# Linear attention with the values as weights and the keys moving on column quarters, products of three steps grouped by tile shape

## The chip, the cores and the metric

The kernel runs on one core of a Trainium2 chip. The metric is the device time of one execution in microseconds (us). Three runs of the kernel before took 985.79, 983.8 and 984.3 us, median 984.3. Engines are named as in the profile: PE (matmul), PEld (weight load, beside PE), DVE, ACT, POOL, and SP, which issues transfers.

## What is computed

Linear attention over 4 batches and 8 heads (576 positions, head size 64, 128 features), then a max-of-three feed-forward layer, then a noisy top-2 mixture of eight experts. Only the attention changes:

```python
def phi(x):
    proj = np.einsum('bhsd,df->bhsf', x, w_phi)
    proj = proj - np.max(np.abs(proj), axis=-1, keepdims=True)
    return np.concatenate([np.exp(proj), np.exp(-proj)], axis=-1)
q_p, k_p = (phi(q), phi(k))
kv = np.einsum('bhsf,bhsd->bhfd', k_p, v)
z = np.sum(k_p, axis=2)
num = np.einsum('bhsf,bhfd->bhsd', q_p, kv)
den = np.einsum('bhsf,bhf->bhs', q_p, z)[..., None] + 1e-06
return (num / den).astype(np.float32)
```

## The kernel before, in words

Attention runs as 16 steps, one for each batch and pair of heads. A step `s` has these parts, each a function:

- `turn` (L388) transposes keys or queries on PE into PSUM, `raw_in` (L398) copies them out on ACT to `th`, and `proj` (L409) multiplies by `w_phi`, 64 rows of the array for each head of the pair. Kind "k" is the keys, "q" the queries, "r" the last 64 positions of two steps together, done on even steps.
- `peak` (L419) and `center` (L434) take the largest absolute value off on DVE, giving `d`. `exp_k` (L446) makes the key features `kp` on ACT. `turn_q` (L452) transposes `d` of the queries on PE, and `exp_q` (L461) makes the query features `qp` from it on ACT.
- `kv_sum` (L481) sums key features times values. The key features are the weights, 128 by 128, and 128 columns move: two value heads of 64, of which one is the ones column block, so that the sum `z` comes out of the same product. One step has 20 such products. `kv_out` (L486) copies the sum to `kv`.
- `denom` (L514) and `numer` (L497) apply it to the query features, 288 positions at a time; `denom` on 32-column quarters of the array, `numer` on 64-column halves.
- `den_in` (ACT), `den_turn` (L529), `den_inv` (L535), `den_copy` (L542), `den_back` (L546) and `divide` (L552, all DVE) end the step and write `xT`.

Beside this, `narrow_mid` (L186, L195 on DVE, L198 on ACT) and `narrow_end` (POOL, four passes) turn 64-bit weights of the next layer into 32-bit ones, 24 halves in all; `narrow_load` (L175) brings their `bits` by DMA.

All order is one list of pairs (time, function), sorted by time: `period` adds the parts of one step at `base + t`, `opening` those before it, and the lines behind `B0` those of the last step, which are mixed with the first products of the next layer (L768). The times are only sort keys. Every engine works its own list in that order, so a waiting instruction holds up all that stands behind it on its engine. PE's results go to eight PSUM banks, named s (3), t (2), p (2) and k (1).

Of the kernel before, what the change touches and what calls it, by code (L numbers as in the profile page):

```python
# [38 lines left out]
def tile_linear_attention__then__moe__then__noisy_top2_moe(  # L39
# [336 lines left out]
    def turn(s, kind):  # L376
# [12 lines left out]
        st["raw", kind] = pt[:, :n]  # L389
# [11 lines left out]
    def proj(s, kind, banks=(bank_p, bank_p)):  # L401
# [3 lines left out]
        pj = [bank().rearrange("p (a f) -> p a f", a=4) for bank in banks]  # L405
# [42 lines left out]
    def turn_q(s, kind, g):  # L448
        pt = bank_t().rearrange("p (a c) -> p a c", a=4)
# [19 lines left out]
    def kv_sum(s, h, part=None):  # L469
        u, i, bb, hp = heads(s)  # L470
        if h == 0 and not part:
            st["pkv"] = bank_k().rearrange("p (a f) -> p a f", a=4)

        order = [(sg, j) for sg in range(2) for j in range(JT)] + [(0, JT), (1, JT)]
        cuts = (0, JT, 2 * JT, len(order))
        for sg, j in order if part is None else order[cuts[part]:cuts[part + 1]]:
            if j < JT:
                kp, vv = kps[s][:, j % 2, 2 * h + j // 2, sg, :], tiles[s][2][:, j, h:h + 2, :]
            else:
                kp, vv = kps[u, "r"][:, h, sg, :], vls[i][:, hp, h:h + 2, :]  # L480
            nc.tensor.matmul(st["pkv"][:, 2 * h + sg, :], kp, vv.rearrange("p a d -> p (a d)"),  # L481
                             start=(j == 0 and sg == 0), stop=(j == JT and sg == 1))

    def kv_out(s):
        kv = ap.tile([P, 4, P], F32, name="kv", bufs=2)
        nc.scalar.activation(kv, st.pop("pkv"), AF.Copy)  # L486
        st["kv", s] = kv

    def numer(s, n, bank=bank_s):
        u, i, bb, hp = heads(s)
        p_ = bank()[:, :HALF]
        for sg in range(2):
            for h in range(2):
                nc.tensor.matmul(p_[h * D:(h + 1) * D], st["kv", s][:, 2 * h + sg, h * D:(h + 1) * D],  # L497
                                 qps[u, i][:, h, sg, n * HALF:(n + 1) * HALF],
                                 start=(sg == 0), stop=(sg == 1))
# [8 lines left out]
    def denom(s, bank=bank_s):  # L508
        u, i, bb, hp = heads(s)
        p_ = bank()[:, :HALF]  # L510
        for sg in range(2):
            for n in range(2):
                for h in range(2):
                    nc.tensor.matmul(p_[quarter(h, n)],  # L514
                                     st["kv", s][:, 2 * h + sg, (1 - h) * D:(1 - h) * D + QD],
# [40 lines left out]
    STEP = 12.5  # L556
# [43 lines left out]
    def period(base, a, b):  # L600

        def at(t, f, *x):
            plan.at(base + t, f, *x)

        if 0 < a < NS:
# [8 lines left out]
        if a < NS and a % 2 == 0:  # L614
            at(0.0, prepare, a)
        if 1 < a < NS:
            if a + 1 == 2 * HP:
                at(0.0, load_rest, 1)
            at(0.0, turn, a, "k")
            at(0.5, raw_in, a, "k")  # L620
            at(2.7, turn, a, "q")
            at(3.2, raw_in, a, "q")
            at(3.15, proj, a, "k")
            at(4.0, peak, a, "k", 0)
            at(4.7, center, a, "k", 0)
            at(5.4, peak, a, "k", 1)
            at(6.1, center, a, "k", 1)
            for g in range(2):
                for sg in range(2):
                    at(5.3 + 1.5 * g + 0.6 * sg, exp_k, a, "k", g, sg)  # L630
            at(7.25, proj, a, "q")
        if 0 < a < NS:
            at(8.1, peak, a, "q", 0)
            at(8.8, center, a, "q", 0)
            at(9.5, peak, a, "q", 1)
            at(10.2, center, a, "q", 1)
            at(9.95, turn_q, a, "q", 0)
            at(10.5, exp_q, a, "q", 0)
            at(11.05, turn_q, a, "q", 1)
            at(11.5, exp_q, a, "q", 1)  # L640
            if a % 2 == 0:
                at(2.8, turn, a, "r")
                at(3.4, raw_in, a, "r")
                at(11.4, proj, a, "r")
                for g in range(2):
                    at(11.5 + 0.01 * g, peak, a, "r", g)
                    at(11.52 + 0.01 * g, center, a, "r", g)
                at(STEP + 3.0, turn_q, a, "r", 0)
                at(STEP + 3.1, exp_q, a, "r", 0)
                at(12.39, exp_k, a, "r", 0, 0)  # L650
                at(12.39, exp_k, a, "r", 0, 1)
        if a < NS:
            for i, n in enumerate(step_halves(a)):
                if i:
                    at(7.6, narrow_high, n)
                    at(11.15, narrow_low, n)
                    at(11.3, narrow_end, n)
                    at(STEP + 4.0, narrow_out, n)
                    continue
                at(1.8 if a > 1 else 11.0, narrow_mid, n)  # L660
                at(2.8 if a > 1 else 11.5, narrow_end, n)
                at(STEP + (1.6 if a > 1 else 9.0), narrow_out, n)
            for n in step_halves(a + 1):
                at(8.0, narrow_load, n)
            if a:
                at(10.5, kv_sum, a, 0, 0)
        if 0 < b:
            at(4.05, numer, b - 1, 1)
            at(6.9, divide, b - 1, 1)
            at(0.45, kv_sum, b, 0, 1)  # L670
            at(2.75, kv_sum, b, 0, 2)
            at(5.0, kv_sum, b, 1)
            if b + 1 == 2 * HP:
                at(7.3, load_rest_v, 1)
            at(7.3, kv_out, b)
        if 0 <= b:
            at(8.15, denom, b)
            at(9.1, numer, b, 0)
            at(9.15, den_in, b)
            at(10.9, den_turn, b)  # L680
            at(11.0, den_inv, b)
            for n in range(2):
                at(11.05, den_copy, b, n)
                at(11.8 + 0.5 * n, den_back, b, n)
            at(11.9, divide, b, 0)

    def opening():

        at(1.2, busy, 12)
        at(4.0, turn, 0, "k")  # L690
        at(4.45, raw_in, 0, "k", True)
        at(4.5, busy, 3)
        at(5.2, proj, 0, "k")
        at(6.3, turn, 0, "r")
        at(6.6, raw_in, 0, "r")
        at(6.6, turn, 0, "q")
        at(7.1, raw_in, 0, "q")
        at(7.2, proj, 0, "r", (bank_s, bank_s))
        at(7.7, proj, 0, "q", (bank_p, bank_s))
        at(9.0, turn, 1, "k")  # L700
        at(9.6, raw_in, 1, "k")
        at(9.7, busy, 4)
        for g in range(2):
            at(6.4 + 1.4 * g, peak, 0, "k", g)
            at(7.1 + 1.4 * g, center, 0, "k", g)
            at(9.3 + 0.01 * g, peak, 0, "r", g)
            at(10.0 + 0.01 * g, center, 0, "r", g)
            at(10.8 + 1.4 * g, peak, 0, "q", g)
            at(11.5 + 1.4 * g, center, 0, "q", g)
            at(13.6 + 1.4 * g, peak, 1, "k", g)  # L710
            at(14.3 + 1.4 * g, center, 1, "k", g)
            for sg in range(2):
                at(8.0 + 1.3 * g + 0.6 * sg, exp_k, 0, "k", g, sg)
                at(15.4 + 2.8 * g + 0.6 * sg, exp_k, 1, "k", g, sg)
        for sg in range(2):
            at(10.7 + 0.4 * sg, exp_k, 0, "r", 0, sg)
        at(11.2, kv_sum, 0, 0)
        at(12.5, turn_q, 0, "r", 0)
        at(12.6, turn, 1, "q")
        at(13.0, exp_q, 0, "r", 0)  # L720
        at(13.2, raw_in, 1, "q")
        at(13.3, proj, 1, "k")
        at(13.8, turn_q, 0, "q", 0)
        at(14.3, exp_q, 0, "q", 0)
        at(14.3, kv_sum, 0, 1)
        at(16.6, kv_out, 0)
        at(16.6, turn_q, 0, "q", 1)
        at(17.1, exp_q, 0, "q", 1)
        at(17.1, proj, 1, "q")
# [3 lines left out]
    for s in range(NS):  # L733
# [1016 lines left out]
```

## Time and profile before

| | us |
|---|---|
| median of three runs | 984.3 |
| the profiled execution's own time | 983.95 |
| its span, first to last instruction | 982.4 |
| PE busy | 972.4 |
| DVE busy | 587.3 |
| ACT busy | 449.7 |
| POOL busy | 489.8 |

The attention takes the first 220 us of the span or so; the two later layers fill the rest. A matmul of 32-bit numbers shows as two records, each with its own weight load, and each lasts longer than the time to the next one's start. So PE's rate is read from starts, not from durations.

### The profile page before, as it was taken

To read this page: it belongs to the slowest core of one execution; us is meant where nothing else is said; L and a number is where in the kernel's file an instruction comes from. 1 tells how busy PE (TensorE), PEld (TensorE's weight loads), DVE (VectorE), ACT (ScalarE), POOL (GpSimd) and SP (SyncE) were. 2 spreads that over 40 slices of the span, in tenths; PEclk is the share of its full clock that TensorE was granted. 3 is DMA by queue.
4 is the path that set the end of the run, shared out by engine and by line. 5 is a ranking of instruction groups with operands and counts; after the bars stand their busy time and mean duration, and the time that the engine had idled before them with its cause. 6 is when DMAs were issued, how large, how long until landed. Compare 5 with 4: busy or idle time off the path is not lost. (4 is left out here: it accounts for less than half of the span.)

```text
span 982.4 us, 17094 instructions
## 1 busy us (share of the span) xinstructions
PE 972.4 (99%) x6285; PEld 852.0 (87%) x6285; DVE 587.3 (60%) x1253; ACT 449.7 (46%) x878; POOL 489.8 (50%) x554
## 2 busy tenths in 40 slices
PE   9999999999999999999999999999999999999997
PEld 7777777779999999999998789989898989889895
DVE  5889888886344363636355525557577665756641
ACT  5666666554233433334335414337364554546350
POOL 2767655582137464545323553137474655647252
PEclk9999999999999999999999999999999999999999
DMA  6547666345155657565516264728475565748312
GB/s 187 147 137 194 186 202 183 119 129 163 47 167 173 220 162 236 176 218 184 178 30 199 55 203 153 293 85 302 143 271 199 203 229 174 279 130 315 113 33 71
DMA packets 125352, 169.08 MB, mean 172 GB/s; under 512 B 35630, under 2 KB 86958, under 8 KB 125266
## 3 DMA queue, kind: packets, MB, share of 16 engines
q1 hardware_dynamic: 114338, 138.35, 45.0%
q0 software_dynamic: 10928, 29.62, 8.7%
q8 instruction: 50, 0.82, 0.3%
q14 instruction: 36, 0.29, 0.1%
HBM read 119.38 MB, written 49.14 MB: 172 GB/s over the span
## 5 line engine op out<-in xcount | busy, mean ns | idle before, releaser
L768 PE MATMUL s<-xh,wh 128*128 128x384 f32 x432 | 147.9, 342 | 0.3 <-DVE a L778 0.3
L768 PE MATMUL s<-xh,wl 128*128 128x384 f32 x432 | 145.3, 336 | 0.0
L768 PE MATMUL s<-xl,wh 128*128 128x384 f32 x432 | 145.1, 336 | 0.0
L1229 POOL DMA_INDIRECT out_dram<-o,emeta x40 | 47.1, 1178 | 130.9 <-DVE o L1227 67.3
L778 DVE TENSOR_TENSOR a<-s,a 128x384 f32<-128x384 f32 x72 | 40.0, 555 | 91.7 <-PE s L768 89.7
L1302 DVE TENSOR_TENSOR wl<-raw,wh 128x1024 fp32r<-128x1024 f32 x58 | 70.8, 1220 | 26.5 <-ACT wh L1294 25.8
L768 PEld LDWEIGHTS s<-xh,wh 128*128 128x128 f32 x432 | 81.1, 188 | 6.2 <-DVE a L778 2.5
L1219 PE MATMUL p<-wh,hh 128*128 128x512 f32 (+1 forms) x216 | 86.4, 400 | 0.0
L1219 PE MATMUL p<-wl,hh 128*128 128x512 f32 (+1 forms) x216 | 85.3, 395 | 0.0
L1219 PE MATMUL p<-wh,hl 128*128 128x512 f32 (+1 forms) x216 | 85.2, 395 | 0.0
L768 PEld LDWEIGHTS s<-xl,wh 128*128 128x128 f32 x432 | 81.2, 188 | 1.5
L768 PEld LDWEIGHTS s<-xh,wl 128*128 128x128 f32 x432 | 81.1, 188 | 0.0
L1294 ACT ACTIVATE wh<-raw 128x1024 fp32r<-128x1024 f32 x58 | 61.2, 1056 | 31.3 <-DMA raw<-in_moe_w_dram 16.5
L1272 POOL TENSOR_TENSOR raw<-raw 128x256 f32<-128x256 f32 x24 | 20.4, 849 | 105.5 <-DMA raw<-in_moe_w_dram 90.5
L481 PEld LDWEIGHTS k<-vt,kp 128*128 128x128 f32 x512 | 60.8, 192 | 6.9 <-issue 6.5
L481 PE MATMUL k<-vt,kp 128*128 128x128 f32 x512 | 66.5, 278 | 0.1
L419 DVE TENSOR_REDUCE m<-p 128x4 f32<-128x512 f32 (+1 forms) x77 | 48.5, 637 | 27.9 <-PE p L409 27.8
L944 POOL DMA_INDIRECT meta<-mt,si x36 | 36.7, 1020 | 56.4 <-DVE si L940 47.3
L206 POOL TENSOR_TENSOR nm<-nm,nr 128x512 int32<-128x512 int32 x24 | 30.5, 1273 | 66.2 <-ACT nr L198 35.2
L1077 PE MATMUL s<-gx,wh 128*128 128x304 f32 x288 | 62.1, 302 | 0.0
L127 DVE TENSOR_TENSOR gx<-t,gx 128x512 fp32r<-128x512 f32 (+3 forms) x82 | 39.5, 496 | 32.9 <-ACT gx L126 32.4
L126 ACT ACTIVATE hh<-a 128x384 fp32r<-128x384 f32 x36 | 18.8, 522 | 87.9 <-DVE a L778 84.6
(279 smaller groups left out, 2552.7 us busy)
## 6 DMA issues: line engine op xcount, KB each, us to landing
raw<-in_moe_w_dram SPq DMA_DIRECT2D x58, 512.0 KB
raw<-in_moe_w_dram SPq DMA_DIRECT2D x48, 256.0 KB
sums<-qh SPq DMA_DIRECT2D x24, 512.0 KB
sums<-raw SPq DMA_DIRECT2D x24, 512.0 KB
wh<-sums SPq DMA_DIRECT2D x24, 512.0 KB
wl<-sums SPq DMA_DIRECT2D x24, 512.0 KB
bits<-in_moe_w_dram SPq DMA_DIRECT2D x18, 512.0 KB
out_dram<-zrow SPq DMA_DIRECT2D x9, 512.0 KB
```

The costliest lines, as they stand in the source:

```text
L127: nc.vector.tensor_tensor(lo, src, hi.bitcast(F32), op=ALU.subtract)
L206: nc.gpsimd.tensor_tensor(m_, m_, r_, op=ALU.add)
L419: nc.vector.tensor_reduce(m, st["pj", kind, g][:, :n], axis=AX.X, op=ALU.max, apply_absolute_value=True)
L481: nc.tensor.matmul(st["pkv"][:, 2 * h + sg, :], kp, vv.rearrange("p a d -> p (a d)"), start=(j == 0 and sg == 0), stop=(j == JT and sg == 1))
L768: nc.tensor.matmul(p_, a[:, d, fs], b_, start=(n == 0), stop=(n == 3 * KD - 1))
L778: nc.vector.tensor_tensor(a, p_, st.pop("a"), op=ALU.max)
L944: ins = nc.gpsimd.indirect_dma_start(out=meta, out_offset=bass.IndirectOffsetOnAxis(ap=si[:, t, kk:kk + 1], axis=0), in_=mt[:, t, kk, :], ...
L1077: nc.tensor.matmul(bk["p"], a[:, d, fs], b_[:, d, :], start=(d == 0 and i == 0), stop=(d == 1 and i == 2))
L1219: nc.tensor.matmul(p_, a, b_[:, fw], start=(f == 0 and r == 0), stop=(f == (3 if seven(n) else F2 - 1) and r == 2))
L1229: alone(e, nc.gpsimd.indirect_dma_start(out=out, out_offset=bass.IndirectOffsetOnAxis(ap=mt[:m, i, 1:2], axis=0), in_=o[:m], in_offset=Non ...
L1294: nc.scalar.activation(WE[e, i][0], st["w2", e, i], AF.Copy)
L1302: nc.vector.tensor_tensor(wl, st.pop(("w2", e, i)), wh.bitcast(F32), op=ALU.subtract)
```

## The change

`kv_sum` now takes 32 columns of the values as weights and moves the key features, 256 columns at a time (both signs), on the four column quarters of the array at once. `z_sum` does the same with 32 columns of ones and 128 moving columns. The result stands turned: `kv_out` copies it to `kvT`, and `kv_turn` (three transposes on PE) and `kv_in` (ACT) turn it back into `kv`. `numer` now works on 32-column quarters, as `denom` did. `period(a)` holds the projections of step a, `turn_q`, `kv_sum` and `z_sum` of step a-1, and `denom` and `numer` of step a-2, each kind of array shape in one run; every PSUM use names its bank. On odd steps from 3 two halves of `narrow` are done instead of on even ones.

```diff
-        pt = bank_t().rearrange("p (a c) -> p a c", a=4)
+        pt = bank(name).rearrange("p (a c) -> p a c", a=4)
...
-            d = ap.tile([P, 4, NF], F32, name="d", bufs=3)
+            d = ap.tile([P, 4, NF], F32, name=f"d{kind}", bufs=2)
...
-        order = [(sg, j) for sg in range(2) for j in range(JT)] + [(0, JT), (1, JT)]
-        cuts = (0, JT, 2 * JT, len(order))
-        for sg, j in order if part is None else order[cuts[part]:cuts[part + 1]]:
-            if j < JT:
-                kp, vv = kps[s][:, j % 2, 2 * h + j // 2, sg, :], tiles[s][2][:, j, h:h + 2, :]
-            else:
-                kp, vv = kps[u, "r"][:, h, sg, :], vls[i][:, hp, h:h + 2, :]
-            nc.tensor.matmul(st["pkv"][:, 2 * h + sg, :], kp, vv.rearrange("p a d -> p (a d)"),
-                             start=(j == 0 and sg == 0), stop=(j == JT and sg == 1))
+    def kv_sum(s):
+        st["pkv"] = bank("k")[:, :3 * P]
+        for j, vv, kp in chunks(s):
+            for c in range(4):
+                h, cs = c // 2, slice(c * QD, (c + 1) * QD)
+                nc.tensor.matmul(st["pkv"][cs, :2 * P], vv[:, 2 * h, c % 2 * QD:(c % 2 + 1) * QD],
+                                 kp[h].rearrange("p g f -> p (g f)"), start=(j == 0), stop=False,
+                                 tile_position=(0, cs.start))
+
+    def z_sum(s):
+        for j, vv, kp in chunks(s):
+            for c in range(4):
+                cs = slice(c * QD, (c + 1) * QD)
+                nc.tensor.matmul(st["pkv"][cs, 2 * P:], vv[:, 1, :QD], kp[c // 2][:, c % 2], start=False,
+                                 stop=(j == JT), tile_position=(0, cs.start))
...
+    def kv_turn(s, name):
+        t = st.pop(("kvT", s))
+        pt = bank(name)[:, :3 * P]
+        for j in range(3):
+            nc.tensor.transpose(pt[:, j * P:(j + 1) * P], t[:, j * P:(j + 1) * P], ident)
...
-            for h in range(2):
-                nc.tensor.matmul(p_[h * D:(h + 1) * D], st["kv", s][:, 2 * h + sg, h * D:(h + 1) * D],
+            for c in range(4):
+                cs = slice(c * QD, (c + 1) * QD)
+                nc.tensor.matmul(p_[cs], st["kv", s][:, sg, cs],
...
-    STEP = 12.5
+    STEP = 10.9
...
-            return min(a, 1) + (a % 2 == 0 or a == NS - 1 if a > 2 else 0)
+            return min(a, 1) + (a % 2 if a > 2 else 0)
...
+        at(0.0, turn, a, "k", A_)
+        at(0.44, turn, a, "q", B_)
+            at(0.88, kv_turn, c, D_)
+        at(1.2, turn_q, b, "q", 0, C_)
+            at(1.65, turn, a, "r", G_)
+        at(1.9, turn_q, b, "q", 1, E_)
+        at(2.35, proj, a, "k", (A_, B_))
+        at(3.25, proj, a, "q", (C_, D_))
+            at(4.15, proj, a, "r", (G_, H_))
+        at(4.6, kv_sum, b)
+        at(6.8, z_sum, b)
+        at(8.0, kv_out, b)
+            at(7.9, denom, c, E_)
+            at(8.9, numer, c, 0, G_)
+            at(9.9, numer, c, 1, H_)
+            den_steps(10.1, c, at)
...
+        at(4.3, turn, 0, "q", C_)
+        at(4.5, turn, 0, "r", G_)
+        at(5.0, proj, 0, "k", (A_, B_))
+        at(5.3, proj, 0, "q", (C_, D_))
+        at(5.5, proj, 0, "r", (G_, H_))
```

The first place where order counts is PE in the middle of the attention. Before, a step with its two turns for "q" stands so (`t<-ident,d` is `turn_q`, `p<-wphi` is `proj`, `k<-v` is `kv_sum`, `s<-qp,kv` is `denom` with 32 and `numer` with 64 columns):

```order
L514 MATMUL s<-qp_160,kv 32x288 x8
L497 MATMUL s<-qp_160,kv 64x288 x4
L452 MATMUL t<-ident,d 128x128 x4
L481 MATMUL k<-vt_110,kp_509 128x128 x4
L452 MATMUL t<-ident,d 128x128 x4
L409 MATMUL p<-wphi,th 128x128 x4
L388 MATMUL t<-ident,km 128x128 x4
L481 MATMUL k<-vt_110,kp_509 128x128 x4
L388 MATMUL t<-ident,qm 128x128 x4
L481 MATMUL k<-vl_111,kp_606 128x128 x2
L452 MATMUL t<-ident,d 128x128 x2
L409 MATMUL p<-wphi,th 128x128 x8
```

Now, from the end of one period to the first projection of the next (L486 is `kv_sum`, L494 `z_sum`, L535 `denom`, L520 `numer`, L392 `turn`, L506 `kv_turn`, L456 `turn_q`, L413 `proj`):

```order
L494 MATMUL k<-kp_516,vt_110 32x128 x16
L494 MATMUL k<-kp_552,vl_111 32x128 x4
L535 MATMUL t_779<-qp_260,kv 32x288 x8
L520 MATMUL s_796<-qp_260,kv 32x288 x8
L520 MATMUL t_813<-qp_260,kv 32x288 x8
L392 MATMUL p_837<-ident,km 128x128 x4
L392 MATMUL p_844<-ident,qm 128x128 x4
L506 MATMUL s_853<-ident,kvT 128x128 x3
L456 MATMUL s_860<-ident,dq 128x128 x4
L392 MATMUL s_874<-ident,kl 128x128
L392 MATMUL s_874<-ident,ql 128x128
L456 MATMUL t_879<-ident,dq 128x128 x4
```

What changed shape seven to nine times in a step changes it three times: 32-column products, transposes, 64-row projections.

The second place is DVE between the last `center` of one step and the first `peak` of the next, before and now:

```order
L434 TENSOR_TENSOR d<-p,m 128x512
L529 STREAM_TRANSPOSE dt<-dn 128x288
L535 RECIPROCAL rc<-dt 128x18
L542 COPY rc<-rc 32x9 x4
L546 STREAM_TRANSPOSE rb<-rc 128x288
L552 TENSOR_TENSOR xT<-s,rb 128x288
L546 STREAM_TRANSPOSE rb<-rc 128x288
L186 TENSOR_SCALAR nm<-bits 128x512
L195 SCALAR_TENSOR_TENSOR nm<-bits,nm 128x512
L419 TENSOR_REDUCE m<-p 128x4
```

```order
L438 TENSOR_TENSOR dq<-s_710,m 128x512
L550 STREAM_TRANSPOSE dt<-dn 128x288
L556 RECIPROCAL rc<-dt 128x18
L563 COPY rc<-rc 32x9 x4
L567 STREAM_TRANSPOSE rb<-rc 128x288
L573 TENSOR_TENSOR xT<-s_796,rb 128x288
L190 TENSOR_SCALAR nm<-bits 128x512
L199 SCALAR_TENSOR_TENSOR nm<-bits,nm 128x512
L567 STREAM_TRANSPOSE rb<-rc 128x288
L573 TENSOR_TENSOR xT<-t_813,rb 128x288
L423 TENSOR_REDUCE m<-p_887 128x4
```

The instructions are the same; both divisions now stand here, where one stood between the key and query projections of the next step.

## Rows read from the trace of the kernel before

**Rows 1.** The page's first part: busy time, share of the span, instructions.

```profile
PE 972.4 (99%) x6285; PEld 852.0 (87%) x6285; DVE 587.3 (60%) x1253; ACT 449.7 (46%) x878; POOL 489.8 (50%) x554
```

**Rows 2.** Windows: length; busy (instructions) of PE, PEld, DVE, ACT, POOL; PEclk, DMA share, GB/s.

```profile
32.49:203.22 170.73, 170.10 (x1643) 132.17 (x1643) 141.97 (x301) 109.68 (x232) 108.31 (x85) 1.00 0.58 166
0.00:12.00 12.00, 9.92 (x79) 7.48 (x80) 5.29 (x13) 5.64 (x11) 6.59 (x34) 1.00 0.48 127
```

**Rows 3.** PE in order of time: start, us, form, records.

```profile
98.70 1.18 PE L514 MATMUL s<-qp,kv 128*32 128x288 f32 x16
99.81 1.19 PE L497 MATMUL s<-qp,kv 128*64 128x288 f32 x8
...
101.42 1.06 PE L481 MATMUL k<-vt,kp 128*128 128x128 f32 x8
102.31 0.60 PE L452 MATMUL t<-ident,d 128*128 128x128 f32 x4
102.76 0.66 PE L388 MATMUL t<-ident,km 128*128 128x128 f32 x4
...
109.98 1.16 PE L409 MATMUL p<-wphi,th 64*128 64x128 f32 x16
111.07 1.18 PE L514 MATMUL s<-qp,kv 128*32 128x288 f32 x16
...
124.83 1.18 PE L514 MATMUL s<-qp,kv 128*32 128x288 f32 x16
```

**Rows 4.** Waits in 32.49 to 203.22 us: total us, times, longest us.

```profile
DVE m L419 <- PE p L409: 22.5, 25, 1.5
```

**Rows 5.** The first of these groups, its second and third set of quarters alone.

```profile
98.97 0.67 PE L514 MATMUL s<-qp,kv 128*32 128x288 f32 x8
...
99.21 0.67 PE L514 MATMUL s<-qp,kv 128*32 128x288 f32 x8
```

**Rows 6.** Groups by line on PEld, 32.49 to 203.22: busy us, mean ns, idle before.

```profile
L514 PEld LDWEIGHTS s<-qp,kv 128*32 128x32 f32 x209 | 5.5, 109 | 4.6
```

**Rows 7.** DVE in order of time, the opening.

```profile
7.13 0.69 DVE L419 TENSOR_REDUCE m<-p 128x4 f32<-128x512 f32 x1 [1.66 <-PE p L409]
...
13.29 0.69 DVE L434 TENSOR_TENSOR d<-s,m 128x512 f32<-128x512 f32 x1
...
26.03 0.48 DVE L546 STREAM_TRANSPOSE rb<-rc 128x288 f32<-128x288 f32 x1
...
27.38 0.53 DVE L186 TENSOR_SCALAR nm<-bits 128x512 int32<-128x512 int32 x1
...
28.55 0.68 DVE L419 TENSOR_REDUCE m<-p 128x4 f32<-128x512 f32 x1
...
31.20 0.45 DVE L552 TENSOR_TENSOR xT<-s,rb 128x288 f32<-128x288 f32 x1
...
35.20 0.47 DVE L529 STREAM_TRANSPOSE dt<-dn 128x288 f32<-128x288 f32 x1
```

**Rows 8.** PE in order of time, the opening.

```profile
5.93 1.16 PE L409 MATMUL p<-wphi,th 64*128 64x128 f32 x16 [0.50 <-ACT th L398]
...
7.53 0.30 PE L388 MATMUL t<-ident,ql 128*128 128x128 f32 x1 [0.18 <-DMA ql<-in_q_dram]
```

**Rows 9.** SP and ACT in order of time: issue of `bits`, and a wait for one.

```profile
16.29 0.61 SPq L175 DMA_DIRECT2D bits<-in_moe_w_dram  x1
...
211.50 0.34 SPq L175 DMA_DIRECT2D bits<-in_moe_w_out_dram  x1
...
215.60 0.69 ACT L198 ACTIVATE nr<-bits 128x512 int32<-128x512 uint32 x1 [0.63 <-DMA bits<-in_moe_w_out_dram]
```

**Rows 10.** PE in order of time, where the next layer begins.

```profile
212.08 0.42 PE L768 MATMUL s<-xh,wh 128*128 128x384 f32 x1
...
214.38 1.18 PE L514 MATMUL t<-qp,kv 128*32 128x288 f32 x16
...
220.00 0.44 PE L768 MATMUL s<-xh,wh 128*128 128x384 f32 x1
```

More of the change, by code (lines that the diff above doesn't have):

```diff
@@ L399, in raw_in, with proj @@
         st["t", kind] = t
-    def proj(s, kind, banks=(bank_p, bank_p)):
+    def proj(s, kind, names):
         t = st["t", kind]
-        pj = [bank().rearrange("p (a f) -> p a f", a=4) for bank in banks]
+        pj = [bank(nm).rearrange("p (a f) -> p a f", a=4) for nm in names]
         for jj in range(2 if kind == "r" else 4):
@@ L506, in quarter, with denom @@
         return slice(g * QD, (g + 1) * QD)
-    def denom(s, bank=bank_s):
+    def denom(s, name):
         u, i, bb, hp = heads(s)
-        p_ = bank()[:, :HALF]
+        p_ = bank(name)[:, :HALF]
         for sg in range(2):
@@ L594, in count, with both, den_steps, loads @@
         def count(a):
-            return min(a, 1) + (a % 2 == 0 or a == NS - 1 if a > 2 else 0)
+            return min(a, 1) + (a % 2 if a > 2 else 0)
         n = sum(count(i) for i in range(a))
         return range(n, n + count(a) if a < NS else len(halves))
-    def period(base, a, b):
-        def at(t, f, *x):
-            plan.at(base + t, f, *x)
+    A_, B_, C_, D_, E_, G_, H_ = "p0", "p1", "s0", "s1", "t0", "s2", "t1"
+    def both(t, kind, a, at):
+        for g in range(2):
+            at(t + 1.4 * g, peak, a, kind, g)
+            at(t + 0.7 + 1.4 * g, center, a, kind, g)
+    def den_steps(t, c, at, last=False):
+        at(t, den_turn, c)
+        at(t + 0.5, den_inv, c)
+        for n in range(2):
+            at(t + 0.8, den_copy, c, n)
+            at(t + 1.5 + 0.9 * n, den_back, c, n)
+            at(t + 2.0 + 0.9 * n, divide, c, n)
+    def loads(a, at):
         if 0 < a < NS:
@@ L613, in period @@
                 at(0.0, load_vals, a + 1)
-        if a < NS and a % 2 == 0:
-            at(0.0, prepare, a)
-        if 1 < a < NS:
             if a + 1 == 2 * HP:
                 at(0.0, load_rest, 1)
[L619 to L651, printed above, removed]
+        if a == 2 * HP:
+            at(7.5, load_rest_v, 1)
@@ L663, in period @@
+                at(2.8 + 0.9 * i, narrow_end, n)
+                at(9.5 + 4.0 * i, narrow_out, n)
             for n in step_halves(a + 1):
                 at(8.0, narrow_load, n)
[L665 to L685, printed above, removed]
+    def period(a):
+        base = a * STEP
+        b, c = a - 1, a - 2
+        def at(t, f, *x):
+            plan.at(base + t, f, *x)
+        loads(a, at)
+        even = a % 2 == 0
+        if not even:
+            at(0.0, prepare, b)
+        at(0.0, turn, a, "k", A_)
+        at(0.1, raw_in, a, "k")
+        at(0.44, turn, a, "q", B_)
+        at(0.5, raw_in, a, "q")
+        if c >= 0:
+            at(0.88, kv_turn, c, D_)
+            at(1.0, kv_in, c)
+        at(1.2, turn_q, b, "q", 0, C_)
+        at(1.3, exp_q, b, "q", 0)
+        if even:
+            at(1.65, turn, a, "r", G_)
+            at(1.7, raw_in, a, "r")
+        at(1.9, turn_q, b, "q", 1, E_)
+        at(2.0, exp_q, b, "q", 1)
+        if not even:
+            at(2.2, turn_q, b, "r", 0, G_)
+            at(3.0, exp_q, b, "r", 0)
+        at(2.35, proj, a, "k", (A_, B_))
+        at(3.25, proj, a, "q", (C_, D_))
+        both(3.4, "k", a, at)
+        for g in range(2):
+            for sg in range(2):
+                at(4.9 + 1.4 * g, exp_k, a, "k", g, sg)
+        if even:
+            at(4.15, proj, a, "r", (G_, H_))
+            for g in range(2):
+                at(6.1 + 0.01 * g, peak, a, "r", g)
+                at(6.12 + 0.01 * g, center, a, "r", g)
+            for sg in range(2):
+                at(7.5, exp_k, a, "r", 0, sg)
+        both(7.4, "q", a, at)
+        at(4.6, kv_sum, b)
+        at(6.8, z_sum, b)
+        at(8.0, kv_out, b)
+        if c >= 0:
+            at(7.9, denom, c, E_)
+            at(8.95, den_in, c)
+            at(8.9, numer, c, 0, G_)
+            at(9.9, numer, c, 1, H_)
+            den_steps(10.1, c, at)
@@ L687, in opening @@
     def opening():
         at(1.2, busy, 12)
[L690 to L702, printed above, removed]
-        for g in range(2):
[L704 to L711, printed above, removed]
+        loads(0, at)
@@ L712, in opening @@
+        at(4.0, turn, 0, "k", A_)
+        at(4.1, raw_in, 0, "k", True)
+        at(4.2, busy, 3)
+        at(4.3, turn, 0, "q", C_)
+        at(4.4, raw_in, 0, "q")
+        at(4.5, turn, 0, "r", G_)
+        at(4.6, raw_in, 0, "r")
+        at(5.0, proj, 0, "k", (A_, B_))
+        at(5.3, proj, 0, "q", (C_, D_))
+        at(5.5, proj, 0, "r", (G_, H_))
+        both(6.0, "k", 0, at)
+        for g in range(2):
             for sg in range(2):
-                at(8.0 + 1.3 * g + 0.6 * sg, exp_k, 0, "k", g, sg)
@@ L714, in opening @@
-                at(15.4 + 2.8 * g + 0.6 * sg, exp_k, 1, "k", g, sg)
+                at(7.0 + 1.4 * g, exp_k, 0, "k", g, sg)
+        for g in range(2):
+            at(9.0 + 0.01 * g, peak, 0, "r", g)
+            at(9.02 + 0.01 * g, center, 0, "r", g)
         for sg in range(2):
[L716 to L729, printed above, removed]
+            at(9.3, exp_k, 0, "r", 0, sg)
+        both(9.3, "q", 0, at)
     at(0.0, start)
     opening()
-    for s in range(NS):
-        period(s * STEP, s, s - 1)
+    for s in range(1, NS):
+        period(s)
     T = NS * STEP
@@ L1410, in first_pe @@
             after(0.6, hidden, c, f)
-    B0 = (NS - 1) * STEP
-    at(B0 + 10.6, open_m1)
     S_ = NS - 1
-    for part in (1, 2):
-        pe(0.65, kv_sum, S_, 0, part)
-    pe(0.96, numer, S_ - 1, 1)
-    at(T + 0.3, split_x, 0, 0)
-    after(0.5, divide, S_ - 1, 1)
-    at(T + 1.6, split_x, 0, 1)
-    pe(2.18, kv_sum, S_, 1)
-    after(0.0, kv_out, S_)
+    at(T - STEP + 4.6, open_m1)
+    pe(0.33, kv_turn, S_ - 1, D_)
+    after(0.0, kv_in, S_ - 1)
+    for g, name in enumerate((C_, E_)):
+        pe(0.44, turn_q, S_, "q", g, name)
+        after(0.0, exp_q, S_, "q", g)
+    pe(2.2, kv_sum, S_)
+    pe(1.1, z_sum, S_)
+    after(0.0, kv_out, S_)
+    pe(1.0, denom, S_ - 1, E_)
+    after(0.0, den_in, S_ - 1)
+    den_steps(clock[0] + 1.5, S_ - 1, at)
+    pe(1.0, numer, S_ - 1, 0, G_)
+    pe(1.0, numer, S_ - 1, 1, H_)
+    at(T + 2.5, split_x, 0, 0)
+    at(T + 3.5, split_x, 0, 1)
     first_pe(0, 0, 0)
-    pe(0.96, denom, S_, bank_t)
+    pe(0.33, kv_turn, S_, E_)
+    after(0.0, kv_in, S_)
+    first_pe(0, 0, 1)
+    pe(1.0, denom, S_, E_)
     after(0.0, den_in, S_)
-    after(0.5, den_turn, S_)
-    after(1.0, den_inv, S_)
-    for n in range(2):
-        after(1.2 + 0.1 * n, den_copy, S_, n)
-        after(1.8 + 0.5 * n, den_back, S_, n)
-    pe(0.96, numer, S_, 0, bank_t)
-    after(1.0, divide, S_, 0)
-    first_pe(0, 0, 1)
-    pe(0.96, numer, S_, 1, bank_p)
-    after(0.6, divide, S_, 1)
+    den_steps(clock[0] + 0.6, S_, at)
+    pe(1.0, numer, S_, 0, A_)
+    pe(1.0, numer, S_, 1, B_)
     for i, n in enumerate(step_halves(NS)):
```

63 lines of the change are left out of this document (32 added, 31 removed).

## Prediction

> **What bounds the kernel now.** I read the page's first part, then the windows, PE in order of time, the waits, and DVE in order of time. PE is busy 99% of the span [rows 1], so the questions are what PE does at each place, and who is next if it does less. The attention is 16 steps. From the `denom` of step 1 at 32.49 us to that of step 14 at 203.22 us lie 13 of them, 170.73 us or 13.13 us each, with PE busy 170.10 us [rows 2]. One step goes from 98.70 to 111.07, the next, with its "r" part, to 124.83 [rows 3]. In the same window DVE waits 22.5 us for the projections on PE [rows 4]. Take that wait away, and DVE still needs (170.73 - 22.5) / 13 = **11.4 us a step**; small gaps and collisions with POOL are in it. So PE is the bound, and DVE stands 1.7 us a step behind it. The change gives DVE the same instructions in another order, so a step can hardly fall below 11.4 us.
>
> **What PE saves in a step.** Eight records of the old `kv_sum` go from 101.42 to 102.31, 0.111 us each [rows 3]; 20 products of two records are 40 x 0.111 = 4.45 us. The new products use quarters, as the old `denom` does. There one set of four quarters starts at 98.97 and the next at 99.21: one record each of four products of 288 columns in 0.24 us [rows 5]. So a set of 256 columns takes 0.215 us. `kv_sum` has 20 products of two records, four at a time: 10 sets, 2.15 us. `z_sum` has 10 sets of 128 columns at 0.108 us, 1.08 us. `kv_turn` is three transposes at 0.11 us (four take 102.31 to 102.76 [rows 3]), 0.33 us. Together 3.56 us, a saving of 0.89 us. No row has a set of 128 columns: the near bound is 0.108 us, and the far one adds a bare weight load of 109 ns to each set [rows 6]. I take the near one, because the sets of rows 5 follow each other at the pace of their columns though they have such loads too.
>
> Next, the changes of shape. `denom` holds four sets, 0.97 us, and yet 1.11 us pass until `numer` starts [rows 3, 5]: 0.14 us for one change. A step has seven or nine of them before and three now, so 5 x 0.14 = 0.7 us go. Taken off 13.13, PE needs 11.5 us. Built up from its pieces it needs less: 21 transposes 2.3, on average 18 projections 2.0 (eight of them and one change take 109.98 to 111.07 [rows 3]), `kv_sum` and `z_sum` 3.2, three groups of 288 columns 2.9, three changes 0.4, in sum 10.9 us. The difference is small waits in the old order that may or may not return.
>
> The Trainium skill, TensorE: Matmul & The Clock Gate, Part 3 (Packing small matmuls), says that a weight load overlaps matmuls in flight only when its row group differs. The quarters here share all rows, so by that rule no load of a next set would be hidden, and each set would be 0.1 us longer. The sets of rows 5 at 0.24 us speak against it for 288 columns; no run here shows it for 128.
>
> **A step after.** DVE needs 11.4, PE 10.9 to 11.5, and each waits for the other once a step. On an even step PE's turn of "r" needs the bank that the first `divide` frees, and the projections stand behind it on PE; DVE's first `peak` needs those projections. From that `divide` on PE needs 2.0 us: six transposes 0.7, a change 0.1, the projection and the way to DVE 1.2 (5.93 to 7.13 [rows 7, 8]). DVE has 2.1 us of work in between: `narrow_mid` 1.2 (27.38 to 28.55) and `den_back` with `divide` 0.9, two thirds of 26.03 to 27.38, which has three instructions of the kind [rows 7]. That just fits. ACT has 109.68 us in 13 steps [rows 2], 8.4 a step, and about 0.4 more for the second copy of `kv`; POOL has 8.3. DVE's 11.4 covers both; they would show only if a step fell to 9. SP issues the same transfers in less time, with the DMA engines at 0.58 of theirs [rows 2], 0.66 then. I take **11.6 us** a step, 0.2 above DVE alone for handoffs that don't fit. Thirteen steps save 13 x (13.13 - 11.6) = **19.9 us**.
>
> **The opening.** `proj` of step 0 now stands behind the turn of "r", which waits for `ql` until 7.53 us; it started at 5.93 before [rows 8]. With the change of shape that is 1.8 us. DVE's first `peak` moves from 7.13 to 8.9, and the end of its last `center` of step 0 from 13.9 (13.29 and 0.6) to 15.7 [rows 7]. Then DVE's list has `narrow_mid` ahead of the next `peak`, and that needs `bits`. SP issues them at 16.29, with the same transfers ahead of them as before; a later one took 4.1 us from its issue at 211.50 to its use at 215.60, where ACT waited for it [rows 9]. So DVE stands still until 20.4, then has 1.2 for `narrow_mid` and 5.3 for keys and queries of step 1 (2.65 for one projection, 28.55 to 31.20 [rows 7]): 26.9. PE then makes 13 transposes, a change and the projection, 2.7 us until DVE starts, and DVE takes 6.7 for keys, "r" and queries: step 2 ends at 36.3. It ended at 35.2 before [rows 7], so **1.1 us** is lost.
>
> PE has little to do while DVE waits for `bits`, and again until 26.9. The granted clock was 1.00, the higher level of 2.4 GHz, even in the first 12 us with PE busy 9.92 [rows 2]. If it fell to 1.2 GHz, the 2.6 us of PE work ahead of DVE's step 2 would double. The bounds are 0 and 2.6; I take **1.0**, nearer to the row at full clock. The Trainium skill, the same page, Part 1 (The HAM clock gate), says that an idle PE drops to half its clock; no row here shows that.
>
> **The end.** At the old spacing step 15's last `center` ends at 35.2 + 170.7 = 205.9, and the third block of the next layer starts at 220.0 [rows 7, 10], 14.1 us later. Now PE has behind that `center`: 11 transposes 1.2, `kv_sum` and `z_sum` 3.2, twice three groups of 288 columns 5.8, two blocks of L768 at 2.2 (212.08 to 214.38 with a change [rows 10]) 4.4, three transposes 0.3, five changes 0.7: 15.6 us, **1.5 more**. From there on PE's work is as before and follows at once.
>
> **Sum.** -19.9 + 1.1 + 1.0 + 1.5 = -16.3. The profiled execution took 983.95 us, 0.35 under the median of 984.3; 983.95 - 16.3 = **967.6 us**.
>
> **Rivals.** (1) *Shorter steps, 961.* PE lands at its 10.9 and DVE collides less with POOL: 11.1 a step saves 26.4, less 3.6 for the ends, 961.2. For it: the lower sum for PE is a plain sum of rows. Against: POOL's same work falls into less time. Chance 0.16.
>
> (2) *The engines wait in turn, 975.* Two nearly equal loads with so tight a handoff leave DVE waiting for projections: at 12.2 a step, 10 of the 22.5 us of wait remain; 12.1 saved, less 3.6, 975.5. The same comes if the 0.14 us between groups is no matter of shape and stays. Chance 0.18.
>
> (3) *Slower: weight loads laid bare, 991.* `kv_sum` and `z_sum` have 20 sets a step. If each waits for its loads of 109 ns [rows 6], PE has 2.2 us more to do: 11.2 + 2.2 = 13.4 a step, 0.27 over now, 3.5 in 13 steps and 3.6 for the ends, 991. It decides from 0.08 us a set, where a step reaches 12.85 and no longer pays for the ends. Against it: rows 5. For it: no row has four quarters with so few columns a set. Chance 0.07. The rule of Part 3 above would bring this case.
>
> **How the numbers follow.** My forecast has a chance of 0.54, and 0.05 stays for mixtures. Forecast, (1) and (2) are all faster; with part of the rest, 0.90. Within 0.2% either way, about what a measurement of this kernel can tell from no change, I put 0.02; slower, with (3), 0.08. The range of 959 to 978 takes in the forecast, (1), (2) and the bounds of the opening, and leaves out (3).
>
> **What would show it.** Right: from one `denom` to the next 11.6 us on average; DVE waits for projections a few us in all where it was 22.5; sets of `kv_sum` follow at 0.215 and of `z_sum` at 0.11 us; DVE stands still for `bits` from 16 to 20 us; the third block of L768 starts at 203.7. Wrong: sets of `z_sum` at 0.2 us or more, a step above 12.5, or a wait for ACT or POOL that ends last on DVE's list.

## The result, and the profile after

The changed kernel takes 991.15 us (median of four runs, 989.62 to 993.33), the kernel before beside it 984.05 (four runs, 983.63 to 985.79): a ratio of 1.007, 95% interval 1.0048 to 1.0093. It is **slower by 0.7%**. The forecast was 967.6 with a range of 959 to 978, and slower had a chance of 0.08. The profiled execution has a span of 991.7 us, 9.3 more than before.

The page's first part, which answers to [rows 1]:

```profile
PE 956.3 (96%) x7225; PEld 832.2 (84%) x7225; DVE 603.9 (61%) x1253; ACT 453.4 (46%) x894; POOL 487.8 (49%) x554
```

PE has 16 us less work, as the change meant, and is idle 25 us more (35.4 us, where it was 10.0). DVE, with the same 1253 instructions, is busy 16.6 us longer. To find the place, I cut the span where DVE starts the first transpose of a step's division (L550, L529 before). Two of these starts, 13 steps apart, from DVE in order of time:

```profile
37.24 0.47 DVE L550 STREAM_TRANSPOSE dt<-dn 128x288 f32<-128x288 f32 x1
...
211.10 0.47 DVE L550 STREAM_TRANSPOSE dt<-dn 128x288 f32<-128x288 f32 x1
```

Before, the first of the two stands at 35.20 ([rows 7]) and the second here; below it is the start of the third block of the next layer on PE, after the change (220.00 before, [rows 10]):

```profile
206.12 0.47 DVE L529 STREAM_TRANSPOSE dt<-dn 128x288 f32<-128x288 f32 x1
```

```profile
227.71 0.45 PE L772 MATMUL s<-xh,wh 128*128 128x384 f32 x1
```

| | before | after | forecast |
|---|---|---|---|
| first of the two starts | 35.20 | 37.24 | 37.3 |
| 13 steps | 170.92 | 173.86 | 150.8 |
| one step | 13.15 | 13.37 | 11.6 |
| from there to the third block of the next layer | 13.9 | 16.6 | 15.6 |
| from there to the end of the span | 762.4 | 764.0 | 762.4 |

The 23 us that are missing lie in the 13 steps. I do not put the last row down to the change: in the twelve experiments, two of them on the kernel before, it lies between 762.0 and 766.3. Its 1.6 us were not traced. The windows of the 13 steps, of a wait in one of them, and of what follows it (columns as in [rows 2]):

```profile
37.24:211.10 173.86, 154.36 (x2405) 114.94 (x2401) 158.04 (x299) 111.23 (x242) 107.50 (x84) 0.94 0.56 164
51.50:55.39 3.89, 0.03 (x1) 0.00 (x1) 3.70 (x7) 1.70 (x4) 2.65 (x3) 0.92 1.12 350
55.39:61.43 6.04, 6.04 (x46) 5.49 (x46) 4.21 (x8) 2.99 (x6) 4.64 (x4) 0.50 0.39 93
```

PE is no longer the bound in the steps (154.36 of 173.86 us), and DVE is busy 12.16 us a step, where the whole step was to take 11.6. PE stands still for 3.9 us in one step, and then works at half its clock. The waits in 37.24 to 211.10 us say who is waited for:

```profile
PEld s L392 <- DVE xT L573: 18.6, 6, 4.1
PE s L392 <- DVE xT L573: 17.2, 6, 3.9
...
DVE m L423 <- PE p L413: 5.8, 5, 1.6
```

DVE's wait for the projections is 5.8 us, as forecast ("a few us", 22.5 in [rows 4]). The new wait is PE's: six times, once in each even step from 4 on, the turn of "r" (L392) waits for the first `divide` (L573), which frees its bank. The case at the start of step 4, on DVE in order of time:

```profile
50.34 0.47 DVE L550 STREAM_TRANSPOSE dt<-dn 128x288 f32<-128x288 f32 x1
50.85 0.27 DVE L556 RECIPROCAL rc<-dt 128x18 f32<-128x18 f32 x1
51.15 3.12 DVE L563 COPY rc<-rc 32x9 f32<-32x9 f32 x4
54.30 0.48 DVE L567 STREAM_TRANSPOSE rb<-rc 128x288 f32<-128x288 f32 x1
54.88 0.46 DVE L573 TENSOR_TENSOR xT<-s,rb 128x288 f32<-128x288 f32 x1
...
56.89 0.46 DVE L573 TENSOR_TENSOR xT<-t,rb 128x288 f32<-128x288 f32 x1
58.97 0.69 DVE L423 TENSOR_REDUCE m<-p 128x4 f32<-128x512 f32 x1 [1.63 <-PE p L413]
```

Four copies of 32x9 numbers take **3.12 us**. Before, four that met nothing took 0.70:

```profile
114.70 0.70 DVE L542 COPY rc<-rc 32x9 f32<-32x9 f32 x4
```

POOL in the same stretch of the changed kernel, and the three slow copies one by one:

```profile
50.18 1.49 POOL L212 TENSOR_SCALAR nr<-nr 128x512 f32<-128x512 f32 x1
51.75 1.27 POOL L213 TENSOR_TENSOR nm<-nm,nr 128x512 f32<-128x512 f32 x1
52.97 1.26 POOL L229 TENSOR_TENSOR wl<-nm,wh 128x512 fp32r<-128x512 f32 x1
```

```profile
51.15 0.54 DVE L563 COPY rc<-rc 32x9 f32<-32x9 f32 x1
...
51.90 1.14 DVE L563 COPY rc<-rc 32x9 f32<-32x9 f32 x1
53.05 1.21 DVE L563 COPY rc<-rc 32x9 f32<-32x9 f32 x1
```

So the first ends at 51.69, the third at 53.04, the fourth at 54.26; POOL's passes end at 51.67, 53.02 and 54.23. The second, 0.17 us at 51.70, starts between two passes. Each slow copy ends when the POOL pass that it met ends. The transpose at 50.34 and the reciprocal at 50.85 lie within POOL's pass of 50.18 and are not slower. The Trainium skill, SBUF — State Buffer, section "Who interferes with whom", says that VectorE and GpSimd share one pair of ports, which one instruction holds to its end while the other stands. It names copies, `tensor_scalar` and instructions with two SBUF inputs, and leaves out those that need the dedicated pair alone. By that rule L563, L190 and L199 stand; the trace agrees, but for a few copies named in the last section.

PE in order of time, with the same projections in the step before for comparison:

```profile
40.83 1.16 PE L413 MATMUL p<-wphi,th 64*128 64x128 f32 x16
41.82 1.06 PE L413 MATMUL s<-wphi,th 64*128 64x128 f32 x16
...
50.93 0.60 PE L456 MATMUL s<-ident,dq 128*128 128x128 f32 x4
55.39 0.47 PE L392 MATMUL s<-ident,kl 128*128 128x128 f32 x1 [3.86 <-DVE xT L573]
55.66 0.42 PE L392 MATMUL s<-ident,ql 128*128 128x128 f32 x1
55.87 1.06 PE L456 MATMUL t<-ident,dq 128*128 128x128 f32 x4
56.86 2.08 PE L413 MATMUL p<-wphi,th 64*128 64x128 f32 x16
58.73 2.12 PE L413 MATMUL s<-wphi,th 64*128 64x128 f32 x17
```

The key projections, queued behind the turn of "r", start late, and at granted clock 0.50 (1.2 GHz) they take 1.87 us (56.86 to 58.73) instead of 0.99. DVE, which was late itself, then waits 1.63 us for them. Such stretches at 0.50 begin at 54.8, 85.5, 112.8, 140.1 and 191.3 us; before, none fell into the attention.

The copies as a group, 0 to 250 us, after and then before:

```profile
L563 DVE COPY rc<-rc 32x9 f32<-32x9 f32 x64 | 26.4, 412 | 1.5
...
L199 DVE SCALAR_TENSOR_TENSOR nm<-bits,nm 128x512 int32<-128x512 int32 x24 | 21.2, 882 | 0.8
L190 DVE TENSOR_SCALAR nm<-bits 128x512 int32<-128x512 int32 x24 | 15.2, 634 | 5.7 <-DMA bits<-in_moe_w_dram 5.7
```

```profile
L195 DVE SCALAR_TENSOR_TENSOR nm<-bits,nm 128x512 int32<-128x512 int32 x24 | 18.7, 778 | 0.7
L542 DVE COPY rc<-rc 32x9 f32<-32x9 f32 x64 | 15.9, 249 | 1.4
...
L186 DVE TENSOR_SCALAR nm<-bits 128x512 int32<-128x512 int32 x24 | 12.2, 509 | 2.8 <-POOL nm L206 2.6 <-DMA narrow<-nm 0.2
```

These three groups, 112 instructions, take 62.8 us where they took 46.8. That is 16.0 of DVE's 16.6 us more. Of the 64 copies, 24 last over 0.3 us where 7 did.

**Theory A**, then: in the new order POOL's passes meet DVE's copies; DVE is late, PE stands in line behind the turn of "r", its clock falls, and DVE waits for it again. **Rivals**: PE's wait in line is a cost of its own, whatever DVE does (B); the place of the two halves is the fault (C); or the quarters on PE are dearer than thought, as the forecast's rival (3) had it, whose 991 the run happens to match.

### The profile page after: what moved, and what is told of

Its sections match the earlier page's. It is cut to its first block, busy times and chain, and to the rows that moved or that the text cites. A ratio compares the mean times of both kernels' runs of the same rounds, so it can differ in the third digit from the quotient of the medians.

```text
span 991.7 us, 19004 instructions
## 1 busy us (share of the span) xinstructions
PE 956.3 (96%) x7225; PEld 832.2 (84%) x7225; DVE 603.9 (61%) x1253; ACT 453.4 (46%) x894; POOL 487.8 (49%) x554
## 5 line engine op out<-in xcount | busy, mean ns | idle before, releaser
L130 ACT ACTIVATE gx<-t 128x512 fp32r<-128x512 f32 (+3 forms) x82 | 34.9, 449 | 44.5 <-DVE t L1056 28.3
L1010 POOL DMA_INDIRECT gx<-x2d,emeta x28 | 28.3, 1011 | 47.9 <-PE t L1020 17.5
L450 ACT ACTIVATE kp<-dk 128x512 f32<-128x512 f32 x64 | 36.9, 629 | 30.3 <-DVE dk L438 30.3
```

Of the source, the lines that this page charges most:

```text
L130: nc.scalar.activation(hi, src, AF.Copy)
L450: nc.scalar.activation(kps[s][:, g, :, sg, :], st["d", kind, g], AF.Exp, scale=scale)
```

## The experiments

Each stands beside runs of the kernel before on the same chip. "Step" is the mean of the 13 steps as cut above. In the expectations of 1, 2 and 4 the letters B and C stand for other rivals, spelled out there: B, that DVE's own longer work sets the step; C, that the low clock alone costs the time.

**1. Another bank for the turn of "r".** It then does not wait for `divide`.

```diff
-            at(1.65, turn, a, "r", G_)
+            at(1.65, turn, a, "r", "k")
```

> Theory A: on odd steps two halves of the weight conversion keep POOL at work while DVE does the four tiny copies; the copies stand until a POOL pass ends, the first divide comes late, PE's turn of the rest waits for its bank (some 4 us), PE's clock falls to 1.2 GHz, the projections take twice as long and DVE waits in turn. Here the turn of the rest goes to bank k, which no divide frees, so the middle of the chain is cut and the copies stay as slow as they are. A expects PE's wait for the divide to be gone, the granted clock 1.00 from step 3 on, DVE's wait for the projections near 0 and about 8 us less than the changed kernel (983). Rival B, DVE's own longer work sets the step and PE's wait only fills time: within 2 us of the changed kernel (990).

986.17 us, ratio 1.0019 (1.0010 to 1.0029), step 13.04. The waits in 37.24 to 211.10:

```profile
PE t L413 <- DVE xT L573: 8.6, 6, 1.5
...
PE s L413 <- DVE xT L573: 3.2, 4, 1.3
```

PE now waits a little later, with the projection of "r" (banks s and t), for the same divisions, and its clock still falls four times in the steps. The copies take 26.7 us, as in the changed kernel. The time lies between the two expectations (983 and 990), and the clock of 1.00 that A expected did not come. DVE no longer waits for the key projections, and yet most of the loss remains: what is late is DVE itself.

**2. The four copies on ACT.**

```diff
-            nc.vector.tensor_copy(rc[quarter(h, 1 - n), n, :], rc[quarter(h, n), n, :])
+            nc.scalar.activation(rc[quarter(h, 1 - n), n, :], rc[quarter(h, n), n, :], AF.Copy)
```

> The four tiny copies of each step go from DVE to ACT, which takes the first link of the chain away and leaves the bank as it is. A expects the first divide 1.3 to 2.3 us earlier on even steps, PE's wait under 2 us there, few or no falls of the clock, and about 15 us less than the changed kernel (976). Rival B (DVE's longer work sets the step) expects the same 13 us that the copies cost DVE in 13 steps, but with the clock falling as before. Rival C, the clock alone costs the time and any wait of PE brings it down: falls as before, at most 5 us less (986).

**968.56 us**, ratio 0.9841 (0.9816 to 0.9865), step 11.60: the forecast's step. The copies as a group on ACT, 0 to 250 us, and the window of the 13 steps:

```profile
L563 ACT ACTIVATE rc<-rc 32x9 f32<-32x9 f32 x64 | 13.4, 209 | 17.5 <-DVE rc L556 16.7
```

```profile
36.33:187.17 150.84, 146.78 (x2413) 108.39 (x2409) 133.18 (x248) 122.08 (x294) 107.28 (x84) 0.99 0.64 191
```

On ACT a copy takes 209 ns on average, and none of the 64 more than 0.21 us, although 47 of them start within a POOL pass. The time is below the 976 that A expected. The 13 steps lose 23.0 us, more than the 21.2 that the copies held on DVE, although DVE still waits 10.1 us for ACT's copies (0 to 250 us): PE's stop and its low clock go with them (one stretch at 0.50 is left in the steps).

**3. No POOL passes.** The four passes of `narrow_end` are left out, and with them the last three bits of the converted weights.

```diff
-        nc.gpsimd.tensor_tensor(m_, m_, r_, op=ALU.add)
-        nc.gpsimd.tensor_tensor(g_, h_, h_, op=ALU.mult)
-        nc.gpsimd.tensor_scalar(g_, g_, TINY * TINY, None, op0=ALU.is_ge)
-        nc.gpsimd.tensor_tensor(o_, o_, g_, op=ALU.mult)
```

> The four POOL passes of narrow_end are left out (the converted weights lack their last three bits); all else is as changed. A expects copies of 0.7 us a step throughout, no wait of PE for the divide above 1 us, clock 1.00 after the opening, a step near 11.4 and about 25 us less than the changed kernel (966). If something other than POOL makes the steps long, the time stays above 980.

962.97 us, ratio 0.9785 (0.9769 to 0.9802), step 11.26. The window, and DVE's copies (L559 here), 0 to 250 us:

```profile
36.36:182.76 146.40, 143.75 (x2405) 106.38 (x2401) 138.13 (x300) 109.86 (x241) 8.91 (x7) 1.00 0.67 198
```

```profile
L559 DVE COPY rc<-rc 32x9 f32<-32x9 f32 x64 | 12.1, 190 | 1.5
```

With the copies on DVE, and PE's order untouched, the whole loss is gone once POOL's four passes are left out. It was not a wait for their results: in the changed kernel's waits from 37.24 to 211.10 DVE never waits for POOL. PE's products are those of the changed kernel, and PE is busy 143.75 / 13 = 11.06 us a step, so rival (3) is out.

**4. PE kept busy during its wait.** Thirty products that nothing reads, ahead of the turn of "r" on even steps.

```diff
+            at(1.6, busy, 30)
             at(1.65, turn, a, "r", G_)
```

> Thirty idle 16-bit matmuls (256 columns, 3.2 us) stand ahead of the turn of the rest on even steps, in bank k; the wait itself stays. It tells the clock's part from the wait's part. C (the clock alone): clock 1.00 from step 3 on, projections at 1.0 us where they took 1.9, about 10 us less (981). A: the same rows, but only the part that DVE waits for the projections comes back, some 6 us (985). B: no change (990).

985.32 us, ratio 1.0014 (1.0004 to 1.0023), step 12.85. The window of the 13 steps, and DVE in the same step 4:

```profile
39.69:206.71 167.02, 164.12 (x2597) 124.14 (x2589) 157.03 (x299) 111.54 (x241) 109.06 (x85) 1.00 0.58 171
```

```profile
53.32 3.12 DVE L563 COPY rc<-rc 32x9 f32<-32x9 f32 x4
```

The clock stays at 1.00, and in this step the copies stand as long as ever. Over the 13 steps 6.8 us of the 23 come back, 0.5 a step. That is the low clock's share only in the rough: DVE's wait for projections falls by 3.5 us (5.8 to 2.3), but its busy time also falls by 1.0, and its waits for `bits` and for `den_in` by 2.3; and at 164.31, where PE had waited only 1.0 us, the thirty products (3.4 us) can hold it up. The rest of the loss, some 16 us, is DVE's.

**5. Edits 1 and 2 together.**

> Both edits: the turn of "r" takes bank k, and the small copies stand on ACT. Theory A (DVE's collisions are the cost, PE's stop a follower): the copies no longer stand, so the first divide is seldom late, and the bank edit adds little to the copies' edit alone, because the projection of "r" still waits for the second divide: 965 to 968, a step of 11.5 or less. Theory B (the in-order wait of PE is a cost of its own): the two parts add, 968.6 less some 5 us: 963 to 964, no wait of PE over 2 us in the steps, no fall of the granted clock.

967.33 us, ratio 0.9828 (0.9811 to 0.9844), step 11.51. It is what A expected; B had 963 to 964. Beside 2 the gain is not resolved. Once the divisions come in time, the bank of "r" hardly matters, so B falls as a cause of its own.

**6. The two halves back on even steps**, copies on DVE.

```diff
-            return min(a, 1) + (a % 2 if a > 2 else 0)
+            return min(a, 1) + (a % 2 == 0 or a == NS - 1 if a > 2 else 0)
```

> The changed kernel with the two halves of narrow back on even steps. If the place of the second half is what brings POOL's run onto the copies (rival C), the even steps lose their collision, the copies fall to some 16 us over 64 and the step to 11.9: 972 to 976. Theory A: the run of POOL takes 10 us of a step of 12 wherever it starts, so it then reaches the divisions of the odd steps; the divisions are as late as before, only the wait for the bank of "r" is met less often: 980 to 988.

979.32 us, ratio 0.9958 (0.9941 to 0.9974), step 12.46, copies 21.5 us over 64, and PE now waits for divisions in `turn_q` (9.1 us in six waits). Neither expectation (972 to 976, 980 to 988): it gives back half of the loss. Where the halves stand decides how many copies POOL meets.

**7. Edits 1 and 2, and the opening's turns of "q" and "r" behind the key projection.**

```diff
-        at(4.3, turn, 0, "q", C_)
+        at(5.1, turn, 0, "q", C_)
...
-        at(4.5, turn, 0, "r", G_)
+        at(5.2, turn, 0, "r", G_)
```

> As the two edits together, and in the opening the turns of "q" and "r" stand behind the projection of the keys, so that the first projection does not wait for the last 64 positions. If DVE's first peak is what moves the opening, it falls from 8.9 us to about 7.2 and the run is 1.5 us shorter than with the two edits alone; if the opening is set by the bits (rival), the first peak moves, step 2's den_turn does not, and the time is within 0.5 us of the two edits alone.

968.07 us, ratio 0.9833 (0.9816 to 0.9849). From DVE in order of time:

```profile
7.55 0.69 DVE L423 TENSOR_REDUCE m<-p 128x4 f32<-128x512 f32 x1 [2.16 <-PE p L413]
...
19.73 0.43 DVE L190 TENSOR_SCALAR nm<-bits 128x512 int32<-128x512 int32 x1 [5.24 <-DMA bits<-in_moe_w_dram]
```

The first `peak` comes 1.4 us earlier than in 5 (8.94), the wait for `bits` ends within 0.2 us of where it did (19.89 in 5), and the first division starts at 37.42 in both. The opening is set by the bits; the time, 0.7 us above that of 5, cannot be told from it.

**8. The kernel before with its copies on ACT**, the edit of 2 at L542.

> The kernel before with only the small copies moved from DVE to ACT. Theory A (these copies collide with POOL only since the two halves and both divisions meet): before, they took 15.9 us over 64, some 250 ns each, and PE was the bound, so nothing is won: 983 to 986, within 0.2% of before. Rival (the copies are slow in any order and the edit is a gain of its own, not a repair of the change): the kernel before gains as well, 970 to 980.

990.1 us, ratio 1.0062 (1.0045 to 1.0079): both expectations missed, it is *slower*. The waits from 36.30 to 211.40:

```profile
DVE m L419 <- PE p L409: 28.5, 27, 1.6
...
PE t L388 <- ACT qp L461: 4.6, 12, 0.5
```

The copies now stand on ACT ahead of the second half of `exp_q`, for which PE's next turn waits: 4.6 us in twelve waits, none of which stands among the waits of before, while the 13 steps are 4.2 us longer (175.10 against 170.92). The projections come later, and PE is the bound: DVE's wait is 28.5 where [rows 4] had 22.5. The same edit wins 23 us in the new order and loses 6 in the old one; it is no gain by itself but the repair of a collision.

**9 to 11. What is left with the copies on ACT.** In 9 `narrow_out` stands at 11.6 instead of 9.5, so that ACT's copies do not stand behind a wait for POOL; 10 is edits 2 and 6; 11 is all three.

```diff
-                at(9.5 + 4.0 * i, narrow_out, n)
+                at(11.6 + 4.0 * i, narrow_out, n)
```

> The copies on ACT, and the last part of a half (the copy of the high word on ACT and the subtraction on POOL) later in the order, so that on ACT the copies do not stand behind a wait for POOL. If that wait (1.7 us at step 4's end, and again later) is what keeps some steps at 13.2 us where their neighbours have 10.6, two of them lose 1.5 us and the time is 965 to 967, against 968.6 with the copies' edit alone. If DVE's own collisions in narrow_mid keep those steps long (rival), under 0.5 us.

> The copies on ACT and the two halves of narrow back on even steps. Theory A (only DVE's collisions count; the copies carry most of it): the halves' place is worth little once the copies are gone from DVE: 965 to 971. Theory C (the place of the second half is a loss of its own, 12 us, and adds to the copies' 22): 957 to 960. If POOL's run on even steps collides with more of DVE's longer instructions, 971 to 975.

> All three: copies on ACT, halves back on even steps, the last part of a half later. Expected by theory A 963 to 970, by theory C 955 to 960, without a step over 13 us but the one that waits for its bits.

967.16 us (0.9801 to 0.9833), 968.0 (0.9814 to 0.9848) and 970.13 (0.9829 to 0.9862). In 9 the step from 73 us falls from 13.2 to 11.6, but its neighbours rise from 10.6 to 11.4. None can be told from 2 and 5. With the copies off DVE the place of the halves is worth nothing: C, worth 12 us in 6, acted through the copies.

**12. The kernel before without POOL's passes**, the edit of 3.

> The kernel before without the four POOL passes of a half in the attention (the last three bits of the converted weights are left out, as in the changed kernel without these passes, which took 963). Theory A (before, PE was the bound and DVE's collisions lay in its waits for projections, so only the changed order pays for them): DVE's copies fall from 15.9 to 12 us, its wait for the projections grows by what it no longer loses, and the time stays at 980 to 984. Rival (POOL's passes cost any order the same): some 28 us less, 953 to 960.

983.2 us, ratio 0.9993 (0.9984 to 1.0003). DVE's wait for projections and its copies (L538 here), 32.49 to 203.22:

```profile
DVE m L415 <- PE p L405: 29.2, 28, 1.5
```

```profile
L538 DVE COPY rc<-rc 32x9 f32<-32x9 f32 x52 | 8.5, 164 | 1.1
```

DVE's work falls by 5.1 us in the window and its wait rises from 22.5 to 29.2. Before, POOL's passes cost nothing because DVE waited for PE anyway; after, the same removal wins 28 us. Theory A stands.

## Why the prediction was wrong

**What held.** PE's saving: the ten sets of `kv_sum` go from 42.81 to 44.99 us (L486, 0.218 a set, forecast 0.215), those of `z_sum` from 44.99 to 46.08 (L494, 0.109, forecast 0.108):

```profile
42.81 1.93 PE L486 MATMUL k<-kp,vt 128*32 128x256 f32 x32
...
44.99 1.06 PE L494 MATMUL k<-kp,vt 128*32 128x128 f32 x32
...
46.08 1.15 PE L535 MATMUL t<-qp,kv 128*32 128x288 f32 x16
```

So the rule of the Trainium skill, TensorE: Matmul & The Clock Gate, Part 3 (Packing small matmuls), that a load overlaps only where the row group differs, does not hold here: these sets share all rows and follow at the pace of their columns. The opening: 37.24 against 36.3 and 1.0 for the clock. `bits` come into use at 19.68 (20.4), and after it the key projection of step 2 takes 1.87 us at granted clock 0.50, 0.9 more than at 1.00. The forecast's clock term (1.0) was right, in the one place where it looked.

**The step that failed**: "Take that wait away, and DVE still needs (170.73 - 22.5) / 13 = 11.4 us a step; small gaps and collisions with POOL are in it." The 11.4 were right for the old order. The step then carried its collisions over to a new order in which the two halves move to odd steps and both divisions, with the four copies, stand together at a step's start. DVE was busy 12.16 us a step, not 11.4 with its gaps, and that is more than the forecast's whole step. The mis-sized term is the collisions: with and without POOL's passes DVE's busy time in the 13 steps is 141.97 and 136.86 us in the old order (experiment 12), 0.4 a step, and 158.04 and 138.13 in the new one (experiment 3), 1.5 a step. What was needed stood in the traces of before: in [rows 2] POOL is busy 63% of the window, and 7 of 64 copies already lasted 0.43 to 1.24 us, each to the end of a POOL pass. The text named "collisions with POOL" as a part of a sum, and did not ask where they would fall.

**The second step**, "That just fits", hung on the first. From the first `divide` PE needed 2.0 us, and DVE had 2.1 us of work: true for PE at full clock (in experiment 4 the next `peak` starts at 59.57, 2.5 us after the first `divide` at 57.06, without a wait). But with the copies 2.4 us late, PE stood for 3.9 us, and then ran at half its clock: from the first `divide` at 54.88 to the next `peak` at 58.97 went 4.1 us. The Trainium skill, TensorE: Matmul & The Clock Gate, Part 1 (The HAM clock gate), says that an idle PE falls to half its clock. The forecast had cited it for the opening alone; the trace agrees in the steps too (0.50 in 55.39 to 61.43). Experiment 4 puts the price at some 0.5 us a step.

**The sum.** Forecast -19.9 for the steps, measured +2.9: the failed term is 22.8 us. The opening was forecast at +2.1 and came out at +2.0. The end was +2.7 instead of +1.5: PE was still 1.2 us behind with `numer` of step 13 when DVE ended its last `center`. With the copies on ACT (experiment 2) the step is 11.60 and the time 968.56, near the forecast. That is in part luck: DVE then no longer has the copies' own work, and still meets POOL in L190 and L199. Without POOL's passes (experiment 3) the step is 11.26, below the 11.4 under which the forecast said it could hardly fall. So the rest of the sum was of the right size, to some 0.3 us a step.

**The rivals.** (3) named 991 and the run gave 991.15, but by another mechanism: no loads are laid bare, and without POOL's passes the same PE program takes 963. A matching total is no evidence for a cause. "A wait for ACT or POOL that ends last on DVE's list" was named as a sign of being wrong, but a collision shows as no wait: only the duration of the instruction grows. The other sign, "a step above 12.5", did come: 13.37.

## What to carry to other kernels

When an order changes, cost each engine's instructions from the rows in which they meet nothing, then add the meetings of the new order: for DVE's copies, its `tensor_scalar` and its instructions with two SBUF inputs, ask what POOL runs at that time. A tiny copy on the path between two engines can cost a whole POOL pass; on ACT it took 209 ns on average, but such a move pays only where ACT is not itself ahead of the bound. And where PE, in order, stands for an engine that is late, count the low clock behind the stop as well (here some 7 us of the 23).

## What was not expected of the hardware

A copy of 32x9 numbers, 0.16 us, lasted up to 1.24 us, and of the 31 that lasted over 0.3 us in the two traces 27 ended within 0.04 us of the end of a POOL pass; the other four met L212 and lasted about 0.5. Not every copy within a pass stands to its end: of the 27 copies that started within a recorded pass in the changed kernel 24 were long; one of the other three met only the last 0.17 us of a pass, and two came at 227.90 and 228.08, in the pass of L212 from 227.24 to 228.72 that had let another copy go after 0.53 us. Spans on POOL are rough, and what in such a pass lets a copy through was not tried. Second, in a kernel whose PE is busy for 96% of its span, the granted clock fell to 0.50 at 54.8 us, within a stop of 3.86 us that ended at 55.39, and the transposes that came next (55.39 to 56.86) ran at 0.50 too.
